# Denominators of linear attention: turned in 32x32 blocks, inverted on 9 columns, and computed inside the next pair's tiled visit

## The chip, the cores and the metric

The kernel runs on one core of a Trainium2 chip. Its engines run side by side, each with an instruction queue of its own that is worked through in order: TensorE (PE in the profile; its weight loads are PEld), VectorE (DVE), ScalarE (ACT), GpSimd (POOL) and SyncE (SP), which here only issues DMA transfers. Engines wait for one another by semaphores. The metric is the device time of one execution in microseconds; the median over runs counts.

## The reference

Two layers follow one another. The first is linear attention over 8 batches, 8 heads, 576 positions and a head size of 64; the second is a layer with a softmax-gated activation and a layer norm.

```python
def phi(x):
    proj = einsum('bhsd,df->bhsf', x, w_phi)               # 64 -> 128 features
    proj = proj - max(abs(proj), axis=-1)
    return concatenate([exp(proj), exp(-proj)], axis=-1)    # 256 features
kv  = einsum('bhsf,bhsd->bhfd', phi(k), v)
z   = sum(phi(k), axis=2)
num = einsum('bhsf,bhfd->bhsd', phi(q), kv)
den = einsum('bhsf,bhf->bhs', phi(q), z) + 1e-06
x   = num / den                                             # 4608 tokens x 512
h   = x @ w_in                                              # 512 -> 1024
solu = h * softmax(h)
out = layer_norm(solu) * g_ln @ w_out                       # 1024 -> 512
```

All of it is in float32 accuracy; large products are split in a high and a low part (names ending in `h` and `l`).

## The kernel before

**Units, pairs and tiles.** The attention is cut in 16 units `u` (a batch has two); a unit holds two pairs of heads (`sub` 0 and 1), so there are 32 pairs. Pair n is `2u + sub`. The second layer is cut in 36 tiles of 128 tokens; the attention of two batches gives nine of them. Tiles of the second layer fill TensorE between the pieces of the attention from about 108 us on, and the last tiles run alone after it.

**One pair.** Keys and queries go through `w_phi` (`pjk`, `pjq`, `pq`), their maximum is subtracted and the exponentials are taken (`ek` for keys, `fq` for queries). A *visit* (`visit`, line 649) is a block of TensorE products in narrow column tiles: `kvT`, the product of key features and v (64 columns wide), and the sums z (32 columns wide). VectorE turns the result (`kv_turn`, tile `kvs`), SP writes it to DRAM (`dk<-kvs`) and reads it back rearranged in four loads (`kvf<-dk`). With `kvf` and `fq` TensorE computes `num` (`q_num`, two PSUM banks of tag `a`) and `den` (`q_den`, line 872, one bank of tag `a`). ScalarE copies `num` out (`E`). For the denominators ScalarE adds 1e-6 while copying (`den_eps`, line 889), VectorE inverts all 128x288 values (`den_recip`, line 893), SP writes four of the rows to DRAM (`d<-dE`, `den_rows`) and reads them back spread over the partitions (`rb<-d`, `den_bcast`), and POOL multiplies (`divide`).

**Joined visits.** From pair `JOIN = 6` on, the visit of a pair begins with `q_num` of the pair before, so that the array changes to narrow tiles once for both. `q_den` is then still an operation of its own, named `qd`, which the planner places where it finds room.

**The order.** A planner (`Plan.order`) lists all operations of all engines with costs, priorities and buffers before the program is built, simulates the five queues and fixes each queue's order. Priorities are sums out of two tables written out in the source, BASE (one entry for each unit or tile) and OFFSET (one for each kind of operation). `START` gives the time at which a queue is free first, `dma` the cost of an issue. The tag `a` has three PSUM banks (`PSUM_BUFS`), which serve `pjk`, `pq`, `mtp`, `mcp`, `num` and `den` by turns. `PORT` names the operations that VectorE and POOL slow each other with. The planner decides the order alone; the engines wait for their real inputs and buffers.

**Start.** POOL fills constants first. The last but one of these are the zeros of `v_half` (tiles `vz`, line 411), into which half tiles of v are loaded; SP's first DMA is such a load.

Of the kernel before, what the change touches and what calls it, by code (L numbers as in the profile page):

```python
# [34 lines left out]
    "den_recip",  # L35
# [17 lines left out]
START = dict(tensor=0.0, vector=950.0, scalar=4000.0, gpsimd=2850.0, sync=600.0)  # L53
# [14 lines left out]
)  # L68
OFFSET = (
# [70 lines left out]
def dma(nbytes, spread=False):  # L140
    return (580 if spread else 400), max(nbytes / 360.0, 50)


class Plan:
# [68 lines left out]
    def order(self):  # L213
# [39 lines left out]
        while len(sequence) < n:  # L253
# [44 lines left out]
            if e == "sync":  # L298
                hold, transfer = o["cost"]
                engine_free[e] = t + hold  # L300
# [56 lines left out]
def linear_attention_then_moe(ctx: ExitStack, tc, qT, qT2, kT, v, w_phi, w_in, g_ln, w_out, out):  # L357
# [19 lines left out]
    def sb(tag, shape, dtype=F32, name=None):  # L377
        return work.tile(shape, dtype, tag=place(tag), bufs=1, name=name or tag)
# [10 lines left out]
    nc = Engines(tc)  # L389
    wph = const.tile([P, 2 * F], F32, name="wph")  # L390
# [19 lines left out]

    v_half = []
    for i in range(NVZ):
        v_half.append(const.tile([P, 2, 2, D], F32, name=f"vz{i}"))
        nc.gpsimd.memset(v_half[i], 0.0)
# [112 lines left out]

    for j in range(2):
        op(("wp", j), "sync", dma(4 * D * F, True), -40 + j, phi_load, (j,))
# [119 lines left out]
    def visit(st, sub, before):  # L649
# [16 lines left out]
        if st["u"] in Z_PE:  # L666
            for g in PARTS[sub]:
                z_mm(st, sub, g, g == PARTS[sub][2])
        else:
            kv_z(st, sub)  # L670

# [217 lines left out]
    def den_eps(st, sub):  # L889
        st["dens", sub] = sb("dE", [P, HC], name="dE")  # L890
        nc.scalar.activation(out=st["dens", sub], in_=st["den", sub][:, :HC], func=AF.Copy, bias=EPS)

    def den_recip(st, sub):
        nc.vector.reciprocal(out=st["dens", sub], in_=st["dens", sub])

    def den_rows(st, sub):
        st["d1", sub] = dram.tile([4, HC], F32, tag="d1", name="d1")
        nc.sync.dma_start(out=st["d1", sub], in_=st["dens", sub][::32, :])
# [393 lines left out]
```

## Time and profile before

| what | value |
|---|---|
| median of 3 runs | 788.21 us (787.93 to 790.29) |
| profiled execution | 793.46 us |
| span in the profile | 791.7 us |
| mean granted TensorE clock | 0.987 |
| TensorE busy | 757.4 us, 96% |
| VectorE busy | 521.6 us, 66% |
| POOL busy | 472.1 us, 60% |
| ScalarE busy | 397.9 us, 50% |

All helper calls are recorded under one line, L345, so work is told apart by its tiles: `den<-fq,kvf` is an instruction that writes `den` and reads `fq` and `kvf`. In a row of the groups, `x32 | 62.0, 1939 | 12.3` means 32 instructions, 62.0 us in all, 1939 ns for one, and 12.3 us in which the engine stood idle just before them, with what ended that. In the chain of waits and in a timeline a row begins with start and length in us.

### The profile page before, as it was taken

The page shows a single profiled execution, that of the slowest core. Times are in us where ns is not written, and L with a number is a line of the kernel's source. Part 1 is how long each engine was busy: PE and PEld are TensorE (multiplying, and loading weights), DVE is VectorE, ACT ScalarE, POOL GpSimd, SP SyncE. Part 2 cuts the span into 40 slices and gives each one's busy share as a digit, 9 for nine tenths or more (in the row PEclk, how much of TensorE's full clock was granted, in tenths as well). Part 3 has the DMA queues.
Part 4 walks back from the last instruction along what each step waited for, and adds up shares of the span by engine and source line. Part 5 has one row for each costly group of instructions (what it writes and reads, how often), then busy time and mean ns, then how long its engine had stood idle before and what let it go on. Part 6 is the DMA issues. An engine that isn't in the chain of part 4 may idle for free. (4 is left out here: it accounts for less than half of the span.)

```text
span 791.7 us, 13472 instructions
## 1 busy us (share of the span) xinstructions
PE 757.4 (96%) x4935; PEld 563.6 (71%) x4935; DVE 521.6 (66%) x797; ACT 397.9 (50%) x782; POOL 472.1 (60%) x507
## 2 busy tenths in 40 slices
PE   4799899999999999999999999999999999899997
PEld 2566567776677767777777777777777776688885
DVE  2998956775776667766567686757668684444343
ACT  2765755464546464464546455553646445222322
POOL 1135679688777579577666866866587846221210
PEclk9899999999999999999999999999999999999999
DMA  6854223243414242343324342423324213100000
GB/s 196 315 175 122 81 69 112 66 139 95 130 35 143 82 138 66 79 147 82 108 70 125 83 123 78 124 63 83 118 79 133 70 28 87 41 27 13 27 28 26
DMA packets 95618, 75.36 MB, mean 95 GB/s; under 512 B 51648, under 2 KB 86080, under 8 KB 95040
## 3 DMA queue, kind: packets, MB, share of 16 engines
q1 hardware_dynamic: 95552, 74.50, 31.9%
q8 instruction: 39, 0.64, 0.4%
q14 instruction: 27, 0.22, 0.1%
HBM read 59.38 MB, written 15.09 MB: 94 GB/s over the span
## 5 line engine op out<-in xcount | busy, mean ns | idle before, releaser
L345 ACT ACTIVATE ek<-dk 128x512 f32<-128x512 f32 (+1 forms) x160 | 86.8, 583 | 62.3 <-DVE dk L345 61.5
L345 PE MATMUL o<-w_out_h,uh 128*128 128x512 f32 x288 | 116.6, 405 | 0.4 <-ACT uh L345 0.4
L345 POOL TENSOR_TENSOR zacc<-zacc,ek 128x512 f32<-128x512 f32 (+1 forms) x78 | 100.8, 1292 | 22.9 <-ACT ek L345 11.9
L345 PE MATMUL o<-w_out_h,ul 128*128 128x512 f32 x288 | 114.2, 397 | 0.0
L345 PE MATMUL o<-w_out_l,uh 128*128 128x512 f32 x288 | 113.9, 396 | 0.0
L345 PE MATMUL h<-win_h,mxh 128*128 128x512 f32 x288 | 93.1, 404 | 1.7 <-DVE eu L345 1.7
L345 PE MATMUL h<-win_l,mxh 128*128 128x512 f32 x288 | 90.4, 395 | 0.0
L345 PE MATMUL h<-win_h,mxl 128*128 128x512 f32 x288 | 90.4, 395 | 0.0
L345 DVE TENSOR_TENSOR ul<-uT,uh 128x512 fp32r<-128x512 f32 x72 | 48.6, 680 | 53.5 <-ACT uh L345 53.5
L345 POOL TENSOR_TENSOR hq<-rawq,hq 64x1152 fp32r<-64x1152 f32 x26 | 69.2, 2661 | 16.5 <-ACT hq L345 11.4
L345 DVE TENSOR_REDUCE nm<-h 128x1 f32<-128x1024 f32 x36 | 43.9, 1219 | 47.8 <-PE h L345 47.8
L345 ACT ACTIVATE fq<-pT 128x576 f32<-128x576 f32 x104 | 67.8, 681 | 14.9 <-DVE pT L345 11.8
L345 PE MATMUL num<-fq,kvf 128*64 128x288 f32 x512 | 70.8, 419 | 3.1 <-ACT eu L345 2.5
L345 ACT CAST uh<-uT 128x512 fp32r<-128x512 f32 x72 | 41.4, 582 | 61.2 <-PE uT L345 52.0
L345 DVE RECIPROCAL dE<-dE 128x288 f32<-128x288 f32 x32 | 62.0, 1939 | 12.3 <-ACT dE L345 12.2
L345 POOL TENSOR_TENSOR blk<-blk,mcol 128x1152 f32<-128x1152 f32 x26 | 55.5, 2135 | 23.1 <-ACT mcol L345 22.9
L345 PE MATMUL kvT<-ek,rawv 128*64 128x256 f32 x512 | 66.8, 394 | 0.0
L345 DVE TENSOR_REDUCE m<-pjk 128x4 f32<-128x512 f32 (+1 forms) x80 | 48.0, 615 | 28.3 <-PE pjk L345 27.9
L345 PEld LDWEIGHTS o<-w_out_h,ul 128*128 128x128 f32 x288 | 54.2, 188 | 13.6 <-DVE ul L345 0.4
L345 PEld LDWEIGHTS h<-win_h,mxl 128*128 128x128 f32 x288 | 54.3, 188 | 12.9
L345 PEld LDWEIGHTS h<-win_l,mxh 128*128 128x128 f32 x288 | 54.1, 188 | 13.0
L345 PEld LDWEIGHTS o<-w_out_h,uh 128*128 128x128 f32 x288 | 54.2, 188 | 11.4 <-ACT uh L345 0.7
(106 smaller groups left out, 1580.2 us busy)
## 6 DMA issues: line engine op xcount, KB each, us to landing
rawq<-in_q SPq DMA_DIRECT2D x26, 576.0 KB
rb<-d SPq DMA_DIRECT2D x64, 144.0 KB
out<-os SPq DMA_DIRECT2D x36, 256.0 KB
rawk<-in_k SPq DMA_DIRECT2D x64, 128.0 KB
rawv<-in_v SPq DMA_DIRECT2D x64, 128.0 KB
dk<-kvs SPq DMA_DIRECT2D x28, 192.0 KB
kvf<-dk SPq DMA_DIRECT2D x112, 48.0 KB
wraw<-in_w_in SPq DMA_DIRECT2D x4, 1024.0 KB
```

Source lines behind the costliest of these rows:

```text
L345: return self.tc.keep_in_program_order(method(*args, **kwargs))
```

## The change

Four things change.

1. `q_den` of the pair before becomes the last part of a joined visit. The visit then takes three `a` banks at once, and the separate operation `qd` remains for pairs 0 to 4 and 31 alone.
2. `den_eps` on ScalarE goes. `den_recip` now has three VectorE instructions: a transpose in 32x32 blocks straight from PSUM, an addition of 1e-6 over every 32nd column (128x9) and a reciprocal of 128x9. Each group of 32 equal rows so becomes 32 different values on 32 partitions. The write to DRAM takes 128 pieces of 9 values where it took 4 rows of 288. `den_recip` leaves `PORT`.
3. POOL writes the zeros of `v_half` ahead of its other constants, and two operations without instructions, `vz` and `set`, tell the planner so; the v halves wait for `vz` in the plan. The planner's cost of a DMA issue rises from 400 to 440 ns, with more for the first 22.
4. BASE and OFFSET are other tables, so every queue has a new order.

```diff
 PORT = (
     "w_bits", "w_in_lo", "w_sum", "w_center", "w_out_lo", "k_lo", "z_add", "q_lo", "q_sub", "divide", "moe_lo",
-    "den_recip",
 )
-START = dict(tensor=0.0, vector=950.0, scalar=4000.0, gpsimd=2850.0, sync=600.0)
+START = dict(tensor=0.0, vector=950.0, scalar=4000.0, gpsimd=1750.0, sync=600.0)
...
-    return (580 if spread else 400), max(nbytes / 360.0, 50)
+    return (580 if spread else 440), max(nbytes / 360.0, 50)
...
                 hold, transfer = o["cost"]
+                hold += 180 if len(dma_done) < 15 else 40 if len(dma_done) < 22 else 0
...
     nc = Engines(tc)
+    v_half = []
+    for i in range(NVZ):
+        v_half.append(const.tile([P, 2, 2, D], F32, name=f"vz{i}"))
+        nc.gpsimd.memset(v_half[i], 0.0)
+
     wph = const.tile([P, 2 * F], F32, name="wph")
...
-    v_half = []
-    for i in range(NVZ):
-        v_half.append(const.tile([P, 2, 2, D], F32, name=f"vz{i}"))
-        nc.gpsimd.memset(v_half[i], 0.0)
...
+    op("vz", "gpsimd", 0, -1e5, lambda: None)
+    op("set", "gpsimd", 1150, -9e4, lambda: None)
...
         else:
             kv_z(st, sub)
+        if before:
+            q_den(*before)
...
-    def den_eps(st, sub):
-        st["dens", sub] = sb("dE", [P, HC], name="dE")
-        nc.scalar.activation(out=st["dens", sub], in_=st["den", sub][:, :HC], func=AF.Copy, bias=EPS)
-
     def den_recip(st, sub):
-        nc.vector.reciprocal(out=st["dens", sub], in_=st["dens", sub])
+
+        flat = sb("dE", [P, HC], name="dE")
+        src = st["den", sub][:, :HC].rearrange("p (t b) -> p b t", b=HC // 32)
+        nc.vector.transpose(out=flat.rearrange("p (b t) -> p b t", t=32), in_=src)
+        c = work.tile([P, HC // 32], F32, tag="cmp", bufs=8, name="cmp")
+        nc.vector.tensor_scalar(out=c, in0=flat[:, ::32], scalar1=EPS, scalar2=None, op0=ALU.add)
+        st["cmr", sub] = work.tile([P, HC // 32], F32, tag="cmr", bufs=8, name="cmr")
+        nc.vector.reciprocal(out=st["cmr", sub], in_=c)
 
     def den_rows(st, sub):
         st["d1", sub] = dram.tile([4, HC], F32, tag="d1", name="d1")
-        nc.sync.dma_start(out=st["d1", sub], in_=st["dens", sub][::32, :])
+        nc.sync.dma_start(out=st["d1", sub].rearrange("q (t b) -> (q t) b", t=32), in_=st["cmr", sub])
...
-                alloc += [("a", ("abs", (pu, "num", ps_, c))) for c in range(2)]
-                early = {(pu, "qv", ps_, c): cost + (1 - c) * 2 * mm32(HC) for c in range(2)}
-                cost += 4 * mm32(HC)
+                alloc += [("a", ("abs", (pu, "num", ps_, c))) for c in range(2)] + [("a", ("abs", (pu, "den", ps_)))]
+                den = 2 * mm32(HC)
+                early = {(pu, "qv", ps_, c): den + cost + (1 - c) * 2 * mm32(HC) for c in range(2)}
+                early[u, "kve", sub] = den
+                cost += 4 * mm32(HC) + den
...
-            add(("de", sub), "scalar", act(HC, True), z + 6.0, den_eps, (sub,), [source["den"]], [("dE", ("dE", sub))],
-                [("den", sub)])
-            add(("dc", sub), "vector", dve(HC) + 30, z + 6.3, den_recip, (sub,), [("de", sub)], (), [("dE", sub)])
-            add(("ds", sub), "sync", (330, 100), z + 6.5, den_rows, (sub,), [("dc", sub)], (), [("dE", sub)])
+            add(("dc", sub), "vector", dve(HC) + 27 + 330, z + 6.3, den_recip, (sub,), [source["den"]],
+                [("dE", ("dE", sub))], [("den", sub)])
+            add(("ds", sub), "sync", (380, 100), z + 6.5, den_rows, (sub,), [("dc", sub)])
```

Left out of the diff are the two tables and the lines that put `qo` and `qd` under the same condition (pairs that are not joined).

More of the change, by code (lines that the diff above doesn't have):

```diff
@@ L960, in linear_attention_then_moe @@
                 for i in range(2):
-                    add(("vl", g, i), "sync", dma(n * 256), z - 3.5, v_half_load, (i,), [("vl", g, 0)] if i else (),
+                    add(("vl", g, i), "sync", dma(n * 256), z - 3.5, v_half_load, (i,), [("vl", g, 0)] if i else [("abs", "vz")],
                         () if i else [("vz", ("rv", g))], [("rv", g)])
@@ L1083, in linear_attention_then_moe @@
             joined = JOIN <= n + 1 < 4 * B
-            source = {"num": ("abs", ((n + 1) // 2, "V", (n + 1) % 2)) if joined else ("qo", sub), "den": ("qd", sub)}
+            visitor = ("abs", ((n + 1) // 2, "V", (n + 1) % 2))
+            source = {"num": visitor if joined else ("qo", sub), "den": visitor if joined else ("qd", sub)}
             if not joined:
@@ L1088, in linear_attention_then_moe @@
                     {(u, "qv", sub, 0): 2 * mm32(HC)})
-            add(("qd", sub), "tensor", 2 * mm32(HC), z + 5.5, q_den, (sub,), feat + [source["num"]],
-                [("a", ("den", sub))], fk)
+                add(("qd", sub), "tensor", 2 * mm32(HC), z + 5.5, q_den, (sub,), feat + [source["num"]],
+                    [("a", ("den", sub))], fk)
             for c in range(2):
@@ L1206, in linear_attention_then_moe @@
     op("tail", "gpsimd", 0, 2 * B * UNIT + 40, start_tail, (),
-       [(2 * B - 1, "qv", s, 1) for s in range(2)] + [(2 * B - 1, "de", s) for s in range(2)])
+       [(2 * B - 1, "qv", s, 1) for s in range(2)] + [(2 * B - 1, "dc", s) for s in range(2)])
     for t in range(NTOK // P):
```

102 rows, old and new, of tables (BASE, OFFSET) are left out of this document.

## The prediction

> **What bounds the kernel now.** I read the busy table and the chain of waits first, then TensorE's waits by releaser, then the busy time by stretch.
>
> ```profile
> span 791.7 us, 13472 instructions
> PE 757.4 (96%) x4935; PEld 563.6 (71%) x4935; DVE 521.6 (66%) x797; ACT 397.9 (50%) x782; POOL 472.1 (60%) x507
> 80.00:100.00 20.00, 16.96 (x141) 10.57 (x141) 18.68 (x22) 15.07 (x34) 14.15 (x9) 0.88 0.30 82
> 440.00:540.00 100.00, 99.72 (x638) 76.03 (x637) 69.33 (x111) 50.57 (x99) 73.58 (x79) 1.00 0.34 93
> ```
>
> In a stretch row the columns are start and end, length, busy time of PE, PEld, DVE, ACT and POOL with instruction counts, granted clock, DMA share and GB/s. TensorE (PE) is busy 757.4 of 791.7 us. From 440 to 540 us it stands still for 0.28 us of 100, so there only fewer or cheaper products shorten the kernel. It loses time in three places: the start; the first 100 us, where VectorE (DVE) is the fuller engine (18.68 of 20 us in the row from 80 to 100); and the end of the attention near 670 us.
>
> **The change part by part.**
>
> *Part 1: denominator products inside the visit (TensorE).* Today `q_den` is an operation of its own. The planner puts some directly behind a visit, when the array is already in its narrow tiles, and some alone between full-width products. The chain of waits shows one of each.
>
> ```profile
> 508.70 1.11 PE den L345 x16
> 509.81 0.74 PE pq L345 x4
> ...
> 527.91 0.97 PE den L345 x16
> 528.88 0.22 PE mtp L345
> ...
> 537.27 0.53 PE pq L345 x4
> ...
> 540.60 2.09 PE num L345 x16
> 542.69 2.51 PE kvT L345 x28
> 545.20 0.22 PE mtp L345
> ```
>
> The columns are start, length, work. A lone group costs 1.11 us, and the four `pq` behind it take 0.74 instead of 0.53: 1.11 + 0.21 = 1.32 us. Behind a visit it costs 0.97, and the `mtp` that follows takes 0.22 whether a den stands between (528.88) or not (545.20). Merging a lone group therefore saves 1.32 − 0.97 = 0.35 us. How many are lone is read from the timeline of PE, where a lone group is drawn 1.18 us long and one behind `kvT` 1.15:
>
> ```profile
> 199.39 1.18 PE L345 MATMUL den<-fq,kvf 128*32 128x288 f32 x16
> ...
> 645.53 1.18 PE L345 MATMUL den<-fq,kvf 128*32 128x288 f32 x16
> 669.14 1.15 PE L345 MATMUL den<-fq,kvf 128*32 128x288 f32 x16
> ```
>
> Of the 26 pairs that are joined to a visit (5 to 30), 13 are lone (first and last row above) and 13 already follow `kvT` (the last of them in the third row). Saving: 13 × 0.35 = **4.5 us**. Everything here is on PE's path, so it counts in full.
>
> *The wait that this part adds.* The visit now takes all three `a` banks: two for `num`, the third for `den`. Behind a `den` that waits for its bank stands all of PE. The bank's last holder is usually a `pjk` product, released by two VectorE instructions over 512 columns, a maximum and this subtraction:
>
> ```profile
> L345 DVE TENSOR_TENSOR dk<-pjk,m 128x512 f32<-128x512 f32 x64 | 43.1, 676 | 0.6
> ```
>
> At 0.68 us each that is 1.35 us, and the `num` and `kvT` of the visit quoted above cover it with 2.09 + 2.51 = 4.6 us. I take 0. With the cover gone it is 1.35 us for each visit that waits (fourth rival).
>
> *Part 2: the reciprocal (ScalarE, VectorE).* Removed are one ScalarE copy and one VectorE reciprocal over 288 columns per pair; added are a transpose over 288 columns, an addition and a reciprocal over 9 columns.
>
> ```profile
> L345 DVE RECIPROCAL dE<-dE 128x288 f32<-128x288 f32 x32 | 62.0, 1939 | 12.3 <-ACT dE L345 12.2
> L345 ACT ACTIVATE dE<-den 128x288 f32<-128x288 f32 x32 | 13.0, 408 | 16.0 <-PE den L345 15.7
> L345 DVE STREAM_TRANSPOSE blk<-pq 128x288 f32<-128x288 f32 x104 | 45.9, 456 | 13.5 <-PE pq L345 12.3 <-issue 0.7 <-DMA kvf<-dk 0.2
> L345 DVE BATCH_NORM_AGGREGATE mv<-bst 128x2 f32<-128x12 f32 x36 | 7.5, 209 | 1.8
> ```
>
> The transpose reads PSUM with a stride here, which no row shows; I take the contiguous 456 ns of the same shape. The 9-column operations are nearest to the 12-column aggregate, 209 ns each. Sum 456 + 418 = 874 ns, so VectorE gains 1939 − 874 = 1065 ns per pair (34 us in all) and ScalarE 408 ns (13 us). From below the new chain is 456 ns and nothing, from above the old 1939 ns. Both engines are off PE's path from 440 to 540, where the saving is hidden by the matrix products and worth 0. It counts in two places.
>
> *Part 2a: end of the attention.* SP issues in order, and the row transfer `d` waits there for the reciprocal ahead of the four `kvf` loads, which the last visits need.
>
> ```profile
> 671.53 1.95 DVE L345 RECIPROCAL dE<-dE 128x288 f32<-128x288 f32 x1 [1.56 <-ACT dE L345]
> 670.00 0.33 SPq L345 DMA_DIRECT2D dk<-kvs  x1
> 673.51 0.56 SPq L345 DMA_DIRECT2D d<-dE  x1
> 674.18 2.60 SPq L345 DMA_DIRECT2D kvf<-dk  x4
> 664.65 2.16 PE L345 MATMUL num<-fq,kvf 128*64 128x288 f32 x16 [0.59 <-DMA kvf<-dk]
> 678.57 3.76 PE L345 MATMUL num<-fq,kvf 128*64 128x288 f32 x16 [2.53 <-ACT eu L345]
> 662.11 2.40 DMA kvf<-dk
> ```
>
> The 2.53 us idle is put down to ScalarE's `eu`, which `num` does not read. The last `kvf` issue ends at 674.18 + 2.60 = 676.78, and 678.57 is 1.8 us later, near the 2.40 us of the chain's `kvf` landing: it was that DMA. `d` was free to go only at 671.53 + 1.95 = 673.48. With the new chain (0.87 us behind the end of `den`, 669.14 + 1.15 = 670.29) it goes at about 671.2 and is done at 671.8. What is late next is the landing of `dk`, 670.33 + 2.40 = 672.7 at the most. So `kvf` starts 674.18 − 672.7 = 1.5 us earlier, and the 0.59 us of the pair before vanishes: **2.1 us**. At best it is 0.59 + 2.53 + 1.6 = 4.7, the last term because the same sixteen products took 3.76 us behind the gap and 2.16 at 664.65. At worst 0.
>
> *Part 2b: the first 100 us.* Four denominators fall there, 4 × 1.07 = 4.3 us of VectorE at most. Only one stands right ahead of a PE wait:
>
> ```profile
> 86.54 1.94 DVE L345 RECIPROCAL dE<-dE 128x288 f32<-128x288 f32 x1
> 90.60 1.13 PE L345 MATMUL pjq<-wph,rawq 128*128 128x256 f32 x4 [0.84 <-DVE dk L345]
> ```
>
> I take that one reciprocal's saving, **1.1 us**; the bounds are 0 and 4.3.
>
> *Part 3: zeros for v first (POOL, SP).* SP's first DMA waits for these zeros, and all other loads stand behind it.
>
> ```profile
> 1.23 0.20 POOL L345 MEMSET ones_mean<- 128x128 f32 x1
> 2.15 0.57 POOL L345 MEMSET vz<- 128x256 f32 x2
> 0.84 0.27 DVE L345 MEMSET wph<- 128x256 f32 x1 [0.84 <-PEq L1282]
> 2.49 0.59 SPq L345 DMA_DIRECT2D vz<-in_v  x1
> 7.24 2.04 PE L345 MATMUL pjk<-wph,rawk 128*128 128x256 f32 x4 [7.24 <-DMA wph<-in_w_phi]
> ```
>
> The zeros move from 2.15 to where `ones_mean` stood, 1.23: 0.9 us earlier. If SP's first entry becomes a load that waits for nothing (the added operation `vz` tells the planner that the v halves come later), SP starts when the engines do, near 0.84: 2.49 − 0.84 = 1.65 us earlier. PE's first product waits for the `wph` load behind it in SP's queue, so it moves with them. I take the middle, **1.3 us**, bounds 0.9 and 1.65.
>
> *Part 4: transfers and order.* `d` is written as 128 pieces of 36 bytes instead of 4 rows. SP's issue was 0.56 us for `d` and 0.33 for the 128-row `dk`, so it may gain 0.2 or lose nothing, off the path. The new BASE and OFFSET move every instruction on every queue. In the steady 100 us there is 0.28 us to gain; a new gap can be lost (third rival). I take 0.
>
> *Sum.* 4.5 + 2.1 + 1.1 + 1.3 = 9.0 us. The profiled execution took 793.46 us for its span of 791.7, so it would become 784.5. The median of the runs is 788.21, 5.25 us under the profiled one; I take the same 9.0 us off it: **779.2 us**. With all best ends it is 4.5 + 4.7 + 4.3 + 1.65 = 15.2 off (773.0), with all worst ends 4.5 + 0.9 = 5.4 off (782.8).
>
> **The rivals.**
>
> *First, the shorter reciprocal is hidden anyway* (parts 2a and 2b are 0): 788.21 − 5.4 = 782.8. For it: PE's waits in the head are for several engines and DMA, and the new order may put other work in these places. Against it: `d` went 0.03 us after the reciprocal ended.
>
> *Second, the change does not do what it says*: a visit that needs three banks is placed later, the 4.5 us of part 1 return as waits for other products, and part 2 is hidden. Then part 3 alone remains, 788.21 − 1.3 = 786.9. Against it: 13 pairs already run in this shape, and their rows show no wait.
>
> *Third, the new order opens a gap with a slow clock behind it.* The one of before:
>
> ```profile
> 90.00:96.00 6.00, 3.20 (x17) 2.37 (x18) 5.99 (x8) 4.76 (x13) 4.45 (x3) 0.94 0.48 148
> 96.00:100.00 4.00, 4.00 (x16) 2.22 (x18) 3.02 (x4) 2.27 (x5) 3.43 (x3) 0.50 0.30 47
> ```
>
> Idle 6.00 − 3.20 = 2.8 us, then 4.0 us of work at clock 0.50 (2.0 lost): 4.8 us in all. One more such place gives 779.2 + 4.8 = 784.0. For it: with a third bank taken by every visit the planner has less to put between. Against it: after 120 us there are whole tiles of `h` and `o` products for filling. The Trainium skill ("TensorE: Matmul & The Clock Gate", What's actually happening) has the clock fall to half after at least one idle window of about 3.4 us. Taken strictly, this gap, half filled, would have cost its idle time alone and the rival would be 779.2 + 2.8 = 782.0; the trace does not agree, since 0.50 was granted behind a stretch with 3.20 us of work in 6.
>
> *Fourth, slower: the third bank.* Every one of the 13 formerly lone groups waits in the visit for its bank, at the full price of 1.35 us: 13 × 1.35 = 17.6 us, 779.2 + 17.6 = 796.8. It decides from (790.6 − 779.2) / 13 = 0.88 us per visit. For it: VectorE is in order and 66% busy, so a release can stand behind a 1.2 us operation. Against it: the cover of 4.6 us.
>
> **How the numbers follow.** Forecast 779.2 with 0.45, hidden reciprocal 782.8 with 0.23, new gap 784.0 with 0.14, no gain from merging 786.9 with 0.08, third bank 796.8 with 0.10. A difference under 0.3% (2.4 us: 785.8 to 790.6) can't be told from none with this kernel. The first two cases and most of the third are faster: 0.45 + 0.23 + 0.11 = 0.79. The rest of the third (0.03) and the second rival (0.08) are about 0.11 for the same, and the fourth is 0.10 for slower. The likeliest case's own range is 773.0 to 782.8. For 8 in 10 I keep its lower end and reach over the third rival and past the second's 786.9, to 787.5.
>
> **What would show it.** Part 1: no group of `den` between full-width products from pair 5 to 30; PE's busy sum 4 to 5 us lower; `den` not waiting in a visit. Part 2: RECIPROCAL over 9 columns at about 0.2 us, transposes of `dE` near 456 ns, VectorE's busy sum about 34 us and ScalarE's 13 us lower. Part 2a: less than 1.6 us of PE idle ahead of the last joined `num`, and no stretch under clock 1.00 behind it. Part 3: PE's first product near 5.9 us. The forecast is wrong if PE's idle sum grows beyond today's 34.3 us (791.7 − 757.4), which the third and fourth rivals would show as a wait ahead of `den` or as a granted clock under 1.00 after 120 us.

## The result, and the profile after

The changed kernel takes 785.01 us in the median (782.84 to 787.79, 8 runs) against 790.49 us for the kernel before, measured beside it. The ratio is 0.9932, with a 95% interval from 0.9907 to 0.9958: 0.68% faster, 5.4 us of 788. The forecast was 779.2, a gain of 9.0. The direction was right, and 3.6 us of the gain are missing (the median itself stands 5.8 us above the forecast, but the kernel before, too, took 2.3 us more than the 788.21 of its first runs). All gains below go by such ratios to the kernel before, times 788.5 us, since the kernel before was measured anew beside each of these kernels and its median differs from time to time.

First the busy table of the changed kernel, whose profiled execution took 785.97 us with a span of 783.9.

```profile
PE 754.0 (96%) x4935; PEld 566.1 (72%) x4935; DVE 500.1 (64%) x861; ACT 384.5 (49%) x750; POOL 471.1 (60%) x507
```

TensorE's busy time fell by 3.4 us and its idle time from 34.3 to 29.9. ScalarE gave 13.4 us, as said; VectorE gave only 21.5 where 34 were forecast. The groups of VectorE's new instructions (busy, mean ns, idle before) hold 5.0 us of the difference, (474 + 340 + 216 − 874) × 32 ns:

```profile
L345 DVE STREAM_TRANSPOSE dE<-den 128x288 f32<-128x288 f32 x32 | 15.2, 474 | 11.0 <-PE den L345 10.9
L345 DVE TENSOR_SCALAR cmp<-dE 128x9 f32<-128x9 f32 x32 | 10.9, 340 | 1.1
L345 DVE RECIPROCAL cmr<-cmp 128x9 f32<-128x9 f32 x32 | 6.9, 216 | 1.1
```

Transpose and reciprocal took about what was forecast (456 and 209 ns). The addition of nine numbers took 340 ns in the mean, more than the reciprocal of the same nine. The busy time by stretch (PE, PEld, DVE, ACT, POOL, granted clock, DMA share, GB/s) tells where the gain went:

```profile
0.00:120.00 120.00, 102.30 (x820) 71.17 (x821) 93.50 (x138) 73.50 (x153) 58.14 (x58) 0.94 0.53 167
...
330.00:350.00 20.00, 17.13 (x106) 12.26 (x105) 12.00 (x21) 10.68 (x19) 14.65 (x17) 0.83 0.40 114
...
660.00:690.00 30.00, 30.00 (x191) 21.63 (x188) 12.62 (x23) 9.43 (x19) 5.41 (x12) 1.00 0.15 41
...
339.00:343.00 4.00, 1.71 (x15) 1.26 (x11) 3.50 (x6) 2.90 (x6) 3.98 (x3) 0.98 0.00 0
343.00:350.00 7.00, 6.42 (x19) 5.25 (x20) 4.96 (x9) 3.89 (x9) 5.90 (x11) 0.52 0.42 96
```

The same stretches of the kernel before:

```profile
0.00:120.00 120.00, 98.33 (x788) 65.69 (x789) 88.41 (x119) 71.90 (x151) 51.52 (x48) 0.93 0.51 160
...
330.00:350.00 20.00, 20.00 (x141) 15.28 (x138) 14.32 (x23) 12.56 (x24) 14.97 (x15) 1.00 0.44 130
...
660.00:690.00 30.00, 26.88 (x167) 18.70 (x167) 12.23 (x16) 10.06 (x20) 12.65 (x14) 0.94 0.23 55
```

The end of the attention gained (30.00 − 26.88) + (1.00 − 0.94) × 30 = 4.9 us. The first 120 us gained as much, (102.30 − 98.33) + (0.94 − 0.93) × 120 = 5.2 us, part of it by the earlier start. But in the middle, where before TensorE was never idle between 330 and 350, there is now a hole with a clock of 0.52 behind it: (20.00 − 17.13) + (1.00 − 0.83) × 20 = 6.3 us lost. Each of these sums compares one profiled execution with one other. These are rows from the timeline of the hole (start, length, engine; in brackets the idle time before and what ended it):

```profile
336.84 1.15 ACT L345 CAST hq<-rawq 128x1152 fp32r<-128x1152 f32 x1 [4.89 <-DMA rawq<-in_q]
...
339.43 1.23 DVE L345 TENSOR_TENSOR eu<-h,eu 128x1024 f32<-128x1024 f32 x1 [4.50 <-ACT eu L345]
340.71 0.66 PE L345 MATMUL uT<-ident,eu 128*128 128x128 f32 x4 [1.47 <-DVE eu L345]
342.02 2.65 POOL L345 TENSOR_TENSOR hq<-rawq,hq 64x1152 fp32r<-64x1152 f32 x1
...
343.06 1.63 DVE L345 TENSOR_SCALAR cmp<-dE 128x9 f32<-128x9 f32 x1
343.08 0.58 PE L345 MATMUL pjk<-wph_h,xh 128*128 128x256 f32 x1 [0.91 <-DVE dE L345]
344.86 0.22 DVE L345 TENSOR_REDUCE mt<-mtp 36x32 f32<-36x128 f32 x1
345.23 0.58 PE L345 MATMUL pq<-hq,w_hh 128*128 128x288 f32 x1 [0.49 <-POOL sa L345]
```

Two things stand in it. ScalarE waits 4.89 us for a half of q (`rawq`), and behind its cast stands `eu`, for which VectorE (4.50 us) and then TensorE's `uT` (1.47 us) wait. And the 128x9 addition lasts 1.63 us instead of 0.17; it ends at 344.69, and GpSimd's `hq`, which began before it, at 344.67. The wait of `pjk` (0.91 us) ends when the transpose ahead of the addition does; only the wait of `pq` (0.49 us) comes behind it. The row puts that one down to GpSimd's `sa`, but `pq` takes a bank of the tag `a` and starts 0.15 us behind the end of `mt` (344.86 + 0.22 = 345.08), which reads such a bank and stands behind the addition in VectorE's queue. The experiments take these apart.

### The profile page after: what moved, and what is told of

It reads as the page before. It is cut to its first block, busy times and chain, and to the rows that moved or that the text cites. A ratio compares the mean times of both kernels' runs of the same rounds, so it can differ in the third digit from the quotient of the medians.

```text
span 783.9 us, 13479 instructions
## 1 busy us (share of the span) xinstructions
PE 754.0 (96%) x4935; PEld 566.1 (72%) x4935; DVE 500.1 (64%) x861; ACT 384.5 (49%) x750; POOL 471.1 (60%) x507
## 4 chain that ended last, share of the span: by engine, by line
PE 55%; DVE 3%; DMA 2%; SPq 1%; ACT 1%; POOL 1%; issue 0%; ACTq 0%; POOLq 0%
PE o L345 18%; PE h L345 17%; PE kvT L345 5%; PE num L345 5%; PE uT L345 3%; PE pjk L345 2%; PE den L345 2%; PE pq L345 2%; DMA rawq<-in_q 2%; SPq L345 1%; DVE bst L345 0%; DVE eu L345 0%; DMA rb<-d 0%; DVE cmp L345 0%; DVE ul L345 0%
## 5 line engine op out<-in xcount | busy, mean ns | idle before, releaser
L345 PE MATMUL num<-fq,kvf 128*64 128x288 f32 x512 | 69.2, 412 | 0.6 <-DMA kvf<-dk 0.6
L345 ACT ACTIVATE eu<-h,nm 128x1024 f32<-128x1024 f32 x36 | 40.2, 1117 | 59.5 <-DVE nm L345 59.1
L345 DVE TENSOR_TENSOR eu<-h,eu 128x1024 f32<-128x1024 f32 x36 | 44.0, 1223 | 36.5 <-ACT eu L345 36.5
L345 PEld LDWEIGHTS h<-win_h,mxl 128*128 128x128 f32 x288 | 54.6, 190 | 13.2
L345 PE MATMUL kvT<-ek,rawv 128*64 128x256 f32 x512 | 64.0, 382 | 0.0
```

The source lines that it names most:

```text
L345: return self.tc.keep_in_program_order(method(*args, **kwargs))
```

## The experiments

**One part alone: the narrow reciprocal.** The order and all operations of the kernel before; only ScalarE's copy and the wide reciprocal are replaced by the three VectorE instructions.

```diff
     def den_eps(st, sub):
-        st["dens", sub] = sb("dE", [P, HC], name="dE")
-        nc.scalar.activation(out=st["dens", sub], in_=st["den", sub][:, :HC], func=AF.Copy, bias=EPS)
+        flat = sb("dE", [P, HC], name="dE")
...
+        nc.vector.transpose(out=flat.rearrange("p (b t) -> p b t", t=32), in_=src)
...
+        nc.vector.tensor_scalar(out=c, in0=flat[:, ::32], scalar1=EPS, scalar2=None, op0=ALU.add)
...
+        nc.vector.reciprocal(out=st["cmr", sub], in_=c)
     def den_recip(st, sub):
-        nc.vector.reciprocal(out=st["dens", sub], in_=st["dens", sub])
+        pass
...
```

Left out are the other lines of these two functions and the write to DRAM, which takes 128 pieces of 9 values here too.

> The kernel before with its own order; only the denominators are turned and inverted as 128x9 (three VectorE instructions where the ScalarE copy stood, no copy, no wide reciprocal). Theory (part 2 is worth its two terms, 2.1 + 1.1 us): 3 us faster than the kernel before, 786 to 788 us beside 790.5, and the PE gap of 2.53 us near 676 us shrinks under 1.0 us. Rival (hidden anyway): within 1 us of the kernel before, the gap stays over 2 us.

Measured: 794.33 us, ratio 1.0066 [1.0043, 1.0090]: slower by 5.2 us, which neither expectation had. The timeline has a new wait of TensorE near 140 us:

```profile
137.65 2.62 POOL L345 TENSOR_TENSOR hq<-rawq,hq 64x1152 fp32r<-64x1152 f32 x1
138.30 0.48 DVE L345 STREAM_TRANSPOSE dE<-den 128x288 f32<-128x288 f32 x1 [3.64 <-PE den L345]
138.82 1.48 DVE L345 TENSOR_SCALAR cmp<-dE 128x9 f32<-128x9 f32 x1
...
140.46 1.29 DVE L345 TENSOR_REDUCE m<-blk 128x36 f32<-128x1152 f32 x1
141.81 0.29 PE L345 MATMUL mtp<-ident,m 128*36 128x128 f32 x1 [2.88 <-DVE m L345]
```

The edit had put the three instructions where ScalarE's copy stood in the order, so VectorE now waits 3.64 us for `den` at the head of its queue, ahead of `m<-blk`. Then the addition lasts until `hq` ends. Place and long addition both are new, so two more kernels separate them.

**The narrow reciprocal in the reciprocal's own place.** ScalarE's copy stays, and with it the moment at which the bank of `den` comes free; VectorE transposes the copy out of SBUF, and no addition is left for it.

```diff
     def den_recip(st, sub):
-        nc.vector.reciprocal(out=st["dens", sub], in_=st["dens", sub])
+        flat = work.tile([P, HC], F32, tag="flat", bufs=2, name="flat")
+        src = st["dens", sub].rearrange("p (t b) -> p b t", b=HC // 32)
+        nc.vector.transpose(out=flat.rearrange("p (b t) -> p b t", t=32), in_=src)
...
+        nc.vector.reciprocal(out=st["cmr", sub], in_=flat[:, ::32])
...
```

> The kernel before with its order, its ScalarE copy and its release of the den bank kept; at the reciprocal's own place in VectorE's queue stand a transpose of 32x32 blocks out of SBUF and a reciprocal of 128x9 (about 0.48 + 0.22 us by the rows of the changed kernel, in place of 1.94), so VectorE should be busy about 40 us less. Theory of parts 2a and 2b: the wait of 2.5 us ahead of the last numerators near 676 us shrinks below 0.5 and the half clock behind it goes: 2.1 to 4.8 us there, and 0 to 1.1 in the first 100 us; 783 to 787 us against 788.9, a ratio of 0.993 to 0.998. Rival, the reciprocal was hidden anyway: within 1 us of the kernel before. Rival, any change of VectorE's times upsets this order as it did when the wait for the den moved to VectorE: 791 to 795 us, with new idle times of TensorE between 120 and 600 us.

Measured: 781.74 us, ratio 0.9914 [0.9883, 0.9945]: 6.8 us faster than before, from this part by itself, and more than any of its expectations had. VectorE's transpose as a group, and the stretches from 120 to 330 us and at the end of the attention:

```profile
L345 DVE STREAM_TRANSPOSE flat<-dE 128x288 f32<-128x288 f32 x32 | 23.0, 718 | 7.5 <-ACT dE L345 7.3
```

```profile
120.00:330.00 210.00, 208.15 (x1386) 155.47 (x1385) 141.28 (x253) 113.58 (x226) 160.85 (x164) 1.00 0.35 101
...
660.00:690.00 30.00, 29.03 (x157) 22.12 (x150) 13.19 (x20) 8.83 (x17) 8.59 (x15) 1.00 0.15 42
```

The kernel before has in the first of these stretches

```profile
120.00:330.00 210.00, 205.42 (x1366) 152.31 (x1364) 147.41 (x238) 112.35 (x223) 159.40 (x164) 1.00 0.34 99
```

At the end it gains (29.03 − 26.88) + 0.06 × 30 = 4.0 us. So most of the wait there was the reciprocal's, through `d` and `kvf`, as part 2a had it; 0.97 us of idle time for `kvf` are left. From 120 to 330 us it gains 208.15 − 205.42 = 2.7 us, where the prediction saw nothing to gain. The rival of a hidden reciprocal falls.

**The same addition out of GpSimd's way.** The kernel of the first experiment (three instructions in ScalarE's place); the addition writes its nine sums as three rows of three, four elements apart. The values are the same.

```diff
-        c = work.tile([P, HC // 32], F32, tag="cmp", bufs=8, name="cmp")
-        nc.vector.tensor_scalar(out=c, in0=flat[:, ::32], scalar1=EPS, scalar2=None, op0=ALU.add)
+        c = work.tile([P, 3, 4], F32, tag="cmp", bufs=8, name="cmp")
+        rows = flat.rearrange("p (a b t) -> p a b t", a=3, t=32)
+        nc.vector.tensor_scalar(out=c[:, :, :3], in0=rows[:, :, :, 0], scalar1=EPS, scalar2=None, op0=ALU.add)
-        nc.vector.reciprocal(out=st["cmr", sub], in_=c)
+        nc.vector.reciprocal(out=st["cmr", sub].rearrange("p (a b) -> p a b", a=3), in_=c[:, :, :3])
```

> The kernel before with the narrow reciprocal alone, the three VectorE instructions in the place of ScalarE's copy (794.3 us against 788.9), and the 128x9 addition now in three rows of three. Theory, the loss was the place: VectorE waits for the den at the head of its queue and what stands behind it comes late; the additions fall to 0.17 us, and the time stays above that of before, 790 to 794 us. Rival, the loss was the additions, 15 of 32 of which were long there (mean 0.66 us, longest 2.14): without them 781 to 786 us, as the kernel with the copy kept had.

Measured: 787.54 us, ratio 0.9964 [0.9944, 0.9985], between both expectations. At the same place of the timeline the wait for `den` is as long as in the first experiment and the addition short:

```profile
137.39 0.48 DVE L345 STREAM_TRANSPOSE dE<-den 128x288 f32<-128x288 f32 x1 [3.64 <-PE den L345]
137.91 0.17 DVE L345 TENSOR_SCALAR cmp<-dE 128x9 f32<-128x9 f32 x1
139.59 0.29 PE L345 MATMUL mtp<-ident,m 128*36 128x128 f32 x1 [1.57 <-DVE m L345]
```

`mtp` waits 1.57 us where it waited 2.88: the 1.31 us less are the 1.48 − 0.17 of the addition. The form of the addition is worth (1.0066 − 0.9964) × 788.5 = 8.0 us in this order. What it stays behind the kernel with the copy kept, (0.9964 − 0.9914) × 788.5 = 3.9 us (uncertainty 2.9), goes with the place of the three instructions: there ScalarE copies nothing and VectorE waits for `den` itself. No run separates these two.

**The changed kernel with the short addition.** Its order is untouched; the edit is the one of the experiment above, of which two lines stand here.

```diff
...
-        nc.vector.tensor_scalar(out=c, in0=flat[:, ::32], scalar1=EPS, scalar2=None, op0=ALU.add)
...
+        nc.vector.tensor_scalar(out=c[:, :, :3], in0=rows[:, :, :, 0], scalar1=EPS, scalar2=None, op0=ALU.add)
...
```

> The changed kernel with its order untouched; only the 128x9 addition writes its nine sums as three rows of three, four elements apart. Theory, the long additions and the late half of q each cost their own: none of the 32 additions over 0.3 us, and 785.0 less the 4.4 us between the two kernels with the half loaded first, 779.5 to 781.5 us; the gap at 339 us (behind the late half) stays, the one of 0.91 us behind it shrinks. Rival, both act on the same stretch and one remedy is enough: 776 to 778 us. Rival, the late half hides the addition's gain: 784 to 786 us.

Measured: 780.19 us, ratio 0.9866 [0.9835, 0.9897], 5.2 us below the changed kernel (uncertainty 3.2). The addition's group, and the place of the hole:

```profile
L345 DVE TENSOR_SCALAR cmp<-dE 128x9 f32<-128x9 f32 x32 | 5.4, 170 | 1.1
```

```profile
335.37 1.15 ACT L345 CAST hq<-rawq 128x1152 fp32r<-128x1152 f32 x1 [5.09 <-DMA rawq<-in_q]
339.24 0.66 PE L345 MATMUL uT<-ident,eu 128*128 128x128 f32 x4 [1.68 <-DVE eu L345]
341.59 0.17 DVE L345 TENSOR_SCALAR cmp<-dE 128x9 f32<-128x9 f32 x1
341.61 0.39 PE L345 MATMUL pjk<-wph_h,xh 128*128 128x256 f32 x1 [0.90 <-DVE dE L345]
```

The part of the hole behind the half of q stays (1.68 us), and so does the wait of `pjk` (0.90 us), which the expectation had shrink: it ends when the transpose ahead of the addition does. The 0.49 us ahead of `pq` are gone; it runs at 342.42, while GpSimd's `hq` still runs to 343.21. The stretch row has no slow clock any more:

```profile
330.00:350.00 20.00, 17.43 (x124) 12.85 (x123) 12.57 (x23) 9.54 (x18) 15.12 (x16) 1.00 0.41 114
```

TensorE is busy only 0.3 us longer here; what returned is the clock. Over all runs the mean granted clock is 0.9908 for the changed kernel and 0.9955 for this one. Clock times span is 775.8 and 774.0 us in the mean, so by this estimate about 1.8 us of the gain are waits (not clear of nothing with an uncertainty of 2.7) and most of it is slow clock that isn't set off.

**The changed kernel without the addition.**

```diff
-        nc.vector.tensor_scalar(out=c, in0=flat[:, ::32], scalar1=EPS, scalar2=None, op0=ALU.add)
...
-        nc.vector.reciprocal(out=st["cmr", sub], in_=c)
+        nc.vector.reciprocal(out=st["cmr", sub], in_=flat[:, ::32])
```

> The changed kernel without the addition of 1e-6 (left out: the reciprocal of the bare sums is taken straight from the transposed block). It takes away the 32 VectorE additions of 128x9, 10.9 us in the profile, of which 10 of 32 last until a GpSimd operation of two inputs ends (up to 1.63 us against 0.17). Theory, VectorE's work is covered: within 1 us of 785.0. Rival, the long additions carry part of the loss in the steady part, since the one of 1.63 us at 343 us stands in front of the gap there: 781 to 783.5 us, and the half clock near 343 us is gone. VectorE's busy time should fall by 11 us in both.

Measured: 779.41 us, ratio 0.9875 [0.9850, 0.9899]. The rival held, with more gain than it had: the additions carry part of the loss. It is no faster than the kernel with the short addition, so no price of the 0.17 us itself can be seen; its waiting had one.

**The half of q that is needed first, loaded first.** The new order issues half 1 of a unit's q directly ahead of half 0 in nine units (4, 5, 8, 9, 11 to 15), though half 0 is cast and used first; the order before had half 0 first in all of them. Here these loads are exchanged on SP's queue, in the changed kernel.

```diff
+    queue = [o["name"] for o in sequence if o["engine"] == "sync"]
+    for u in range(3, 2 * B):
+        late, soon = (u, "ql", 1), (u, "ql", 0)
+        if soon in queue and 0 < queue.index(soon) - queue.index(late) < 3:
+            o = sequence.pop(sequence.index(plan.ops[plan.index[late]]))
+            sequence.insert(sequence.index(plan.ops[plan.index[soon]]) + 1, o)
```

> The changed kernel with one thing else: where SP issues the two query loads of a unit next to each other, the half that is needed first is issued first (9 units); every other queue keeps its order. Theory (the stretch near 340 us is lost because the half needed first lands 7.7 us after its issue, behind the other half): ScalarE's wait for rawq near 332 us falls from 4.9 us to under 2.5, the PE gaps of 1.47, 0.91 and 0.49 us from 338 to 345 us and the slow clock behind them go, and the kernel is 2 to 5 us faster than the changed one, 780 to 783 us. Rival (both halves share the bandwidth whatever their order, or VectorE's 1.63 us addition makes the gap): the wait stays over 4 us or the gaps stay, 784 to 787 us.

Measured: 780.90 us, ratio 0.9887 [0.9857, 0.9918], 3.5 us below the changed kernel (uncertainty 3.1, so barely clear of nothing).

```profile
336.04 1.15 ACT L345 CAST hq<-rawq 128x1152 fp32r<-128x1152 f32 x1 [2.96 <-DMA rawq<-in_q]
340.30 0.66 PE L345 MATMUL uT<-ident,eu 128*128 128x128 f32 x4
342.27 1.65 DVE L345 TENSOR_SCALAR cmp<-dE 128x9 f32<-128x9 f32 x1
344.45 0.37 PE L345 MATMUL pq<-hq,w_hh 128*128 128x288 f32 x1 [1.20 <-POOL sa L345]
```

ScalarE waits 2.96 us instead of 4.89 (under 2.5 was expected) and `uT` not at all; the addition is still 1.65 us long. The gaps did not all go: TensorE still waits 0.51 us ahead of `pjk`, and ahead of `pq`, which starts 0.15 us behind the end of `mt` here too, 1.20 us where it was 0.49. But the clock stayed at 1.00 in this execution. ScalarE's waits for `rawq` as a whole (us, times, longest) were, for the kernel before,

```profile
ACT hq L345 <- DMA rawq<-in_q: 8.0, 6, 2.5
```

for the changed kernel,

```profile
ACT hq L345 <- DMA rawq<-in_q: 15.4, 8, 4.9
```

and here

```profile
ACT hq L345 <- DMA rawq<-in_q: 10.0, 6, 3.0
```

**Both remedies.** The exchanged loads and the addition in rows of three.

> The kernel with the first needed half of q loaded first (780.9 us), and in it the 128x9 addition writes its nine sums as three rows of three, four elements apart, where it wrote nine in a row. Theory, the addition waits for GpSimd because it runs in a mode that uses two ports, and rows of an odd length spaced apart take it out of this mode: no addition over 0.3 us, mean near 0.18 us (against 0.34), VectorE 5 us less busy, and a time of 778.5 to 780.5. Rival, the mode depends on the plain shape read, which is the same: additions of over 1 us remain, and the time is within 1 us of 780.9.

Measured: 776.45 us, ratio 0.9837 [0.9808, 0.9865], 12.9 us below the kernel before, the fastest of all and 2 us better than expected. No addition is long (minimum, median and maximum in ns), and the hole is gone:

```profile
L345 DVE TENSOR_SCALAR cmp<-dE x32: 166/170/174, 37.3 to 675.7; 128x9 f32<-128x9 f32 x32
```

```profile
330.00:350.00 20.00, 19.63 (x143) 14.42 (x141) 13.05 (x25) 11.00 (x22) 19.09 (x20) 1.00 0.29 78
```

With the two alone at 5.2 and 3.5 us, both give 12.9 − 5.4 = 7.5 us over the changed kernel: they nearly add up. The times by themselves do not tell the two remedies together from the short addition alone (2.3 us apart, uncertainty 3.3); the timelines do. With the loads exchanged the wait behind the addition is left (1.20 us ahead of `pq`), with the short addition the wait behind the half of q is left (1.68 us ahead of `uT`), and with both neither is. So there are two waits and not one.

**A leave of the narrow tiles inside each joined visit.** One full-width transpose of the identity into an unused part of the `kvT` bank, between the sums of `z` and `den`, in 26 visits. It is an added product, and nothing is left out.

```diff
                 z_mm(st, sub, g, g == PARTS[sub][2])
         else:
             kv_z(st, sub)
         if before:
+            nc.tensor.transpose(out=kv[:, 3 * F : 4 * F], in_=ident, identity=ident)
             q_den(*before)
```

> The changed kernel with one full-width transpose of the identity matrix (an extra product of about 0.11 us whose result nobody reads) between the sums and the denominators of each of the 26 joined visits, so that the array leaves its narrow tiles and comes back once more per visit. Theory (a lone group costs 0.35 us more for leaving and entering narrow tiles): 26 x (0.35 + 0.11) = 12 us slower than the changed kernel, about 797 us, and each visit is 0.4 to 0.5 us longer in the trace. Rival (the switch itself is cheap, and the lone groups were long for what stood beside them): 26 x 0.11 = 3 us, about 788 us.

Measured: 792.56 us, ratio 1.0050 [1.0028, 1.0071], 9.3 us above the changed kernel. One visit of this kernel, and the same in the changed kernel:

```profile
507.30 0.43 PE L345 MATMUL kvT<-zacc,ones 128*32 128x128 f32 x8
507.66 0.33 PE L345 MATMUL kvT<-ident 128*128 128x128 f32 x1
507.92 1.18 PE L345 MATMUL den<-fq,kvf 128*32 128x288 f32 x16
```

```profile
502.10 0.43 PE L345 MATMUL kvT<-zacc,ones 128*32 128x128 f32 x8
502.34 1.15 PE L345 MATMUL den<-fq,kvf 128*32 128x288 f32 x16
```

From the `z` sums to `den` it is 0.62 us instead of 0.24: 0.38 us more. By the time it is 9.3 / 26 = 0.36 us, with an uncertainty of 0.1. Less the 0.11 of the product itself that the expectation gave (the four such transposes of `uT` begin at 340.71 and the next product at 341.20, 0.12 each), a leave and return costs 0.25 to 0.27 us; the 0.35 of part 1 lies at the edge of the uncertainty. The figure of the timeline is the cleaner one: in this execution the additions took 21.7 us where they took 10.9, so the time holds other waits too.

**The old wide reciprocal in the new order.** Addition and reciprocal on VectorE over 288 columns, no transpose.

```diff
-        nc.vector.transpose(out=flat.rearrange("p (b t) -> p b t", t=32), in_=src)
...
-        nc.vector.tensor_scalar(out=c, in0=flat[:, ::32], scalar1=EPS, scalar2=None, op0=ALU.add)
...
-        nc.vector.reciprocal(out=st["cmr", sub], in_=c)
+        st["dens", sub] = sb("dE", [P, HC], name="dE")
+        nc.vector.tensor_scalar(out=st["dens", sub], in0=st["den", sub][:, :HC], scalar1=EPS, scalar2=None, op0=ALU.add)
+        nc.vector.reciprocal(out=st["dens", sub], in_=st["dens", sub])
...
```

> The changed kernel with its own order; only the inversion is again 128x288 wide, both steps on VectorE (an addition of about 0.4 us and a reciprocal of 1.94 us per pair, some 1.5 us more of VectorE per pair than the narrow form, 48 us in all). Theory (VectorE's time is off PE's path for most of the run, and counts at the start and at the end of the attention): 3 to 6 us slower than the changed kernel, 788 to 791 us. Rival (in the new order the narrow form is hidden everywhere): within 1.5 us of the changed kernel, 784 to 786.5. Other rival (the banks that visits now fill are released late, so VectorE counts at each visit): over 10 us slower.

Measured: 803.89 us, ratio 1.0175 [1.0139, 1.0210], 19 us above the changed kernel, a time that only the expectation's last rival covers. VectorE's two groups, and a stretch of the steady part in which TensorE was busy 206.88 of 210 us in the changed kernel:

```profile
L345 DVE RECIPROCAL dE<-dE 128x288 f32<-128x288 f32 x32 | 62.5, 1953 | 1.1
L345 DVE TENSOR_SCALAR dE<-den 128x288 f32<-128x288 f32 x32 | 14.3, 448 | 11.3 <-PE den L345 11.1
```

```profile
120.00:330.00 210.00, 201.14 (x1322) 150.28 (x1322) 143.52 (x233) 103.08 (x199) 152.04 (x156) 1.00 0.33 94
```

With 2.40 us per pair instead of 1.03, this order isn't covered: 5.7 us more idle time in this stretch alone. From 120 to 660 us TensorE's `pq` waits 4.9 us in six places for VectorE's `mt`, which reads a bank of the tag `a`; the changed kernel has no such wait. This is the rival's mechanism, banks that are released late. So VectorE is on the path of the steady part when it is late by a microsecond or so.

**The zeros for v written late,** where the kernel before writes them, in the changed kernel's order.

> The changed kernel, with the zeros for v written where the kernel before writes them (behind the other constants in GpSimd's queue). Theory of part 3: the first v load waits for them, and the loads behind it with it; TensorE's first product goes from 5.0 back to about 7.2 us and the time rises by 1.3 to 2.2 us over the changed kernel, to 786.3 to 787.2. Rival, the first 100 us are held by transfers and by ScalarE and the early start is waited away by 30 us: first product at 7.2, time within 0.7 us of 785.0.

Measured: 785.02 us, ratio 0.9956 [0.9934, 0.9978]. The ratio is 1.9 us above the changed kernel's with overlapping intervals, the medians are equal: not to be told from nothing. TensorE's first product came at

```profile
6.08 2.05 PE L345 MATMUL pjk<-wph,rawk 128*128 128x256 f32 x4 [6.08 <-DMA wph<-in_w_phi]
```

and in the changed kernel at

```profile
5.03 2.04 PE L345 MATMUL pjk<-wph,rawk 128*128 128x256 f32 x4 [5.03 <-DMA wph<-in_w_phi]
```

It did not go back to 7.24, as the expectation had it: of the 2.2 us earlier start about 1.05 are the zeros', the rest goes with the new order on SP, which issues two loads that wait for nothing ahead of them (from 0.72 us on).

## Why the prediction was right or wrong

**Part 1 (4.5 us): held as far as it could be tried.** After 120 us each of the 26 joined visits has its `den` inside. The price of a leave and return came out at 0.25 to 0.27 us beside the 0.35 assumed, so the 13 groups are worth 3.3 to 4.5 us. That merging by itself gives this was not shown, since the merged operations have no order among the old tables.

**The added wait (0 us): right,** and with it the fourth rival falls. The group of all `den` products has hardly any idle time before it (its last number). The one bank that came late (`pjk` at 343.08, 0.91 us) stands behind the visit and waited for VectorE, late because of q.

```profile
L345 PE MATMUL den<-fq,kvf 128*32 128x288 f32 x512 | 37.0, 407 | 0.3 <-ACT E L345 0.3
```

**Part 2, durations: right but for one, and that is the first step that failed.** "The 9-column operations are nearest to the 12-column aggregate, 209 ns each" gave the addition a fixed price from an instruction that GpSimd does not hold up (the aggregate took 208 to 211 ns in all 36 places). The addition measured 0.17 us alone and up to 1.63 us while a GpSimd operation with two inputs over 512 or more columns ran: ten of 32 took over 0.2 us, and each of the nine whose GpSimd operation can be told apart ended 0.02 to 0.04 us behind it. In rows of three it took 0.17 us at 341.59 although `hq` ran from 340.55 to 343.21. The long additions cost 5.2 us (the changed kernel with the short addition). The change had also taken `den_recip` out of `PORT`, so the planner placed the addition without regard to GpSimd. The Trainium skill ("SBUF — State Buffer", Who interferes with whom) has the rule: VectorE's `tensor_scalar` can run in a mode that needs the pair of ports it shares with GpSimd, and whichever of the two comes second is blocked until the first is done. The trace agrees: the addition at 343.06 ends 0.02 us behind `hq`, and the reciprocal, of the same 128x9, is never over 0.22 us. That rule spoke against this change, and I had not weighed it. That the port is the cause is the page's reading; the runs show that the long additions end with GpSimd's work and vanish with another form of the output.

**Part 2, its worth: wrong.** "Both engines are off PE's path from 440 to 540, where the saving is hidden" was read from the best 100 us and used for the whole of 120 to 660 us. In the kernel before TensorE stood still for 210 − 205.42 = 4.6 us between 120 and 330, a fourth place of loss beside the three that the prediction names. The saving is worth 6.8 us in the old order (parts 2a and 2b had 3.2), its lack in the new order costs 19 us, and the long additions cost 5.2: VectorE counts between 120 and 440 us.

**Part 2a (2.1 us): right mechanism, too small.** It measured 4.9 us by the stretch in the changed kernel and 4.0 with the narrow reciprocal alone, near the best end of 4.7: the slow clock behind the gap went as well. In the changed kernel `d` goes 0.02 us behind the reciprocal, and the loads of `kvf` follow from 666.94 on:

```profile
666.11 0.22 DVE L345 RECIPROCAL cmr<-cmp 128x9 f32<-128x9 f32 x1
...
666.35 0.32 SPq L345 DMA_DIRECT2D d<-cmr  x1
```

**Part 2b (1.1 us):** not measured by itself; the clock of the first 120 us differs too much among executions.

**Part 3 (1.3 us): the start came 2.2 us earlier, its worth is open** (0 to 1.9 us).

**Part 4 (0 us): the second step that failed.** "...a new gap can be lost (third rival). I take 0." The new order brought the halves of q in the wrong order in nine units, worth 3.5 us (uncertainty 3.1). This is the third rival's mechanism, a gap with a slow clock behind it, and its 784.0 is the number nearest to 785.0. But its ground was another: no lack of work between visits with three banks, but a late load and a late addition. The first rival's 782.8 is what the ratio gives (788.21 × 0.9932 = 782.9), and yet the reciprocal was not hidden: a right number by luck, from two errors that nearly cancel. The Trainium skill's rule, as the prediction took it strictly ("TensorE: Matmul & The Clock Gate", What's actually happening), again did not fit: 0.52 was granted behind 1.71 us of work in 4, with no idle piece longer than 1.47.

The sum: 6.8 for the reciprocal, 3.3 to 4.5 for the merging and 0 to 1.9 for the zeros make 10.1 to 13.2 us, and the kernel with both faults mended measured 12.9 [10.6, 15.1]. Less 5.2 and 3.5 the changed kernel would gain 1.4 to 4.5; it gained 5.4 [3.3, 7.3]. This agrees within the uncertainty, if the 6.8 us of the old order hold in the new one, which no run shows. So the forecast missed by 3.6 us only because two errors worked against each other: the reciprocal's worth was put 3.6 us too low, and two losses of 7.5 us together were put at nothing.

## What to carry to other kernels

A saving on an engine that is 65% busy is not worth nothing because one stretch hides it: look at the worst stretches, and ask what stands behind the instruction in its queue. Price a small instruction also by what may hold it up: here nine sums waited up to 1.6 us for another engine, and writing them in another shape gave back 5.2 us, more than the 3.6 that were missing. With a new order look at the loads in pairs: is the one that is needed first also issued first?

## What the runs showed that was not expected

- A 128x9 addition from SBUF to SBUF takes 0.17 us, or as long as GpSimd's running two-input operation (1.63 us at 343 us, 2.14 at the longest in the first experiment, 2.63 in the kernel with the leave). Written as three rows of three it took 0.174 us at most. Which property of the shape decides it is open.
- The 32x32 transpose of 128x288 in the same stride took 474 ns out of PSUM and 718 ns out of SBUF (671 at the least, so not by waiting now and then). No run tells why.
- In the profiled execution of the changed kernel the clock fell to half for about 7 us after a stretch in which TensorE was half idle: 1.71 of 4 us busy from 339 to 343, and then 0.52. In that of the short addition, with 0.3 us more work in the 20 us around, it did not fall. Here the clock cost more, 0.17 × 20 = 3.4 us, than the 2.9 us of the gaps themselves. It does not fall there in every execution: one execution of the changed kernel (783.42 us) has a mean clock of 0.997 over a span of 781.5 us, which leaves 0.003 × 781.5 = 2.3 us for all its slow clock together. What decides it is open.
